# Moving the loads of the weights' chunks from SyncE's DMA queue to GpSimd's

## The chip, the cores and the metric

The kernel runs on one core of one Trainium2 chip. Its time is the device time of one execution in microseconds (us); the median of several executions counts. TensorE (PE) multiplies matrices, VectorE (DVE) and ScalarE (ACT) work on elements, GpSimd (POOL) does some element work too, and SyncE (SP) does nothing but issue DMAs. Each engine takes its instructions strictly in the order in which the program put them: an instruction that waits holds up all that stand behind it on that engine.

## What is computed

Four batches of eight attention heads (576 positions, 64 wide) with a rotation of queries and keys by position (rope), and on the attention's output, as 2304 tokens of 512, a gated layer of 1536 hidden columns:

```python
q_rot, k_rot = (rotate(q), rotate(k))
scores = scale * np.matmul(q_rot, k_rot.transpose(0, 1, 3, 2))
attn = softmax(scores); out = np.matmul(attn, v)
x = out, heads side by side: (2304, 512)
gate = 1.0 / (1.0 + np.exp(-(x @ w_gate)))
return (gate * (x @ w_val) @ w_out)
```

All is float32 at the interface. The kernel splits most operands into two float16 parts (a rounded part and what is left of it) and multiplies the parts.

## The kernel before

The weights come as 64-bit words, made of float32 pairs, that must be decoded on the chip: `w_in_chunk(f)` loads chunk f of w_gate and w_val (12 chunks, 1024 KB each) into one of three staging slots inside the tile `wo16`, decodes it with two ACT passes (`signs` L286, `low_bits` L291) and three DVE passes (`bits_1` L295, `bits_2` L298, `bits_3` L302), measures it (L324) and splits it into `w16` (L275 on ACT, L281 on DVE). `w_out_decode(f)` does the same for 12 chunks of w_out (512 KB each) through two buffers `tmp`, which lie inside `xt[1]`, the second batch's buffer.

Attention runs over a batch, four pairs of heads (p = 0 to 3) and two halves of the query rows (i = 0, 1). `keys_queries(b, p)` loads a pair's keys and queries (`x`, in the tiles `stk` for the first two batches and `qk` for the others) and the same with halves exchanged (`y`, in one of two tiles `sw`), and rotates them by two multiplications and an addition (L416, L418, L420) for each of keys and queries: on DVE for batches 0 and 1, on POOL for batches 2 and 3. `softmax` takes scores from PE (L470 for the first two batches), scales and reduces them on DVE (L505), exponentiates on ACT (L510), takes reciprocals (L513, L515) and splits the result into `p16` (L275, L281). SP then transposes `p16` into `pt` by a DMA (L537), for the last 64 rows after a small copy (L534), and PE multiplies `pt` with the values into `pv` (L547). ACT and DVE take `pv` into `xt` (L275, L281), and DVE reduces `xt` to a maximum (L556). `hidden(b, f, i)` multiplies the tokens in `xt` with a chunk of `w16` (L598), `project` with w_out (L632).

All 12 chunks of w_in and the attention of batch 0 must be done before PE can run the rest without pause: with the second half of batch 0 (i = 1) the multiplications of L598 become 320 columns wide, and the first of these marks the end of the opening.

The order on every engine is written by `Plan`. Each step is a task with an engine, a cost, a rank, and the names of what it reads and writes; a task that reads or writes a name waits in the plan for the task that last wrote it. `Plan.order` runs a list schedule over these costs, always the ready task of least rank on the engine that is free first, and the instructions are then emitted in that sequence. The waits on the chip are put in separately, from the tiles that instructions touch: a name in the plan sets only the order. A DMA is a task of SP with 0.45 us (`dma`, L224) that lands after a bus time; `port` is the plan's model of what DVE and POOL may not do at once. The first three loads of w_in and the first two of w_out need nothing but free slots.

Of the kernel before, what the change touches and what calls it, by code (L numbers as in the profile page):

```python
# [13 lines left out]
I32 = mybir.dt.int32  # L14
# [20 lines left out]
class Plan:  # L35
# [27 lines left out]
    def order(self):  # L63
        N = len(self.tasks)
        succ = [[] for _ in range(N)]
        left = [len(p) for p in self.preds]
        for n, p in enumerate(self.preds):
            for m in p:
                succ[m].append(n)
        free, wait, ready, done = {}, {}, {}, [None] * N  # L70

        def offer(n):
            for e, _ in self.tasks[n][0]:
                t = 0.0
                for m in self.preds[n]:
                    e0, end, land = done[m]
                    t = max(t, end if e0 == e and not land else end + land + self.HOP)
                heapq.heappush(wait.setdefault(e, []), (t, self.tasks[n][1], n))
                ready.setdefault(e, [])
                free.setdefault(e, 0.0)  # L80

        for n in range(N):
            if not left[n]:
                offer(n)
        starts, bus, port = [], 0.0, 0.0
        while len(starts) < N:
            best = None
            for e in free:
                w, r = wait[e], ready[e]
                while w and done[w[0][2]]:  # L90
                    heapq.heappop(w)
                while r and done[r[0][1]]:
                    heapq.heappop(r)
                if r or w:
                    t = free[e] if r else max(free[e], w[0][0])
                    if best is None or t < best[0]:
                        best = (t, e)
            t, e = best
            w, r = wait[e], ready[e]
            while w and w[0][0] <= t:  # L100
                _, rank, n = heapq.heappop(w)
                if not done[n]:
                    heapq.heappush(r, (rank, n))

            held = e in ("DVE", "POOL") and port > t + 0.2
            fit = [x for x in r if not held or (e == "DVE" and not self.tasks[x[1]][4])]
            if fit:
                x = min(fit)
                r.remove(x)
                heapq.heapify(r)  # L110
            else:
                x = heapq.heappop(r)
            n = x[1]
            where, rank, fn, land, locks = self.tasks[n]
            cost = dict(where)[e]
            if e == "POOL" or (e == "DVE" and locks):
                t = max(t, port)
                port = t + cost
            if land:

                bus = max(bus, t + cost) + land[0]
                done[n] = (e, t + cost, bus + land[1] - t - cost)
            else:
                done[n] = (e, t + cost, 0.0)
            free[e] = t + cost
            starts.append((t, n, e))
            for m in succ[n]:
                left[m] -= 1
                if not left[m]:
                    offer(m)  # L130
        self.done = done
        return sorted(starts)
# [24 lines left out]
def rope_attention_then_sigmoid_glu(ctx: ExitStack, tc: tile.TileContext, qk, v, w_in, w_out, tables, out):  # L157
    nc = tc.nc
    V, A, G, T, Y = nc.vector, nc.scalar, nc.gpsimd, nc.tensor, nc.sync
# [29 lines left out]
    tmp = [xt[1].rearrange("p c a n -> p (c a n)").bitcast(I32)[:, 1152 * n:1152 * n + 1152] for n in range(2)]  # L189
# [18 lines left out]
    P = Plan()  # L208
# [15 lines left out]
    def dma(rank, reads, writes, kb, fn, also=()):  # L224
        P.add((("SP", 0.45),), rank, reads, writes, lambda _: fn(), land=(kb / 280, 1.6), also=also)

    def transpose(rank, reads, writes, us, fn):
        P.add((("SP", 1.3),), rank, reads, writes, lambda _: fn(), land=(us, 1.2))

# [77 lines left out]
    def w_in_chunk(f, rank):  # L307
        slot = ring("stage", 3)
        tok = [("wo", 4 * slot + n) for n in range(4)]
        t = stage[slot]  # L310
        hi, lo = t[:, :, 1], t[:, :, 0]
        dst = w16[:, f].rearrange("p g a c n -> p g a (c n)")
        sg = w16[:, f, 1].rearrange("p a c n -> p (a c n)").bitcast(I8)[:, 1024:2048]
        W = ("w", f)
        dma(rank - 0.15, [], tok, 1024, lambda: Y.dma_start(out=t.rearrange("p n w -> p (n w)"), in_=w_in[f].bitcast(I32)))
        op("ACT", c_act(1024), rank, tok, [W], lambda E: signs(sg, hi))
        op("ACT", c_act(1024), rank, [], tok, lambda E: low_bits(lo))
        op2(0.7, rank, [W], tok, lambda E: bits_1(hi, hi))
        op2(c_dve(1024, two=True), rank, [], tok, lambda E: bits_2(hi, lo))
        op2(c_dve(1024, two=True), rank, [W], tok, lambda E: bits_3(hi, sg))  # L320
        r = hi.bitcast(F32).rearrange("p (g n) -> p g n", g=2)
        M = ("wm", f)
        for g in range(2):
            op("ACT", c_act(512) + 0.2, rank, tok, [M, W], lambda E, g=g: A.activation(  # L324
                dst[:, g, 0], r[:, g], AF.Abs, accum_out=w_m[:, f, g:g + 1]))
        place = m_place()
        top = allsum(rank, w_m[:, f], 2, place, [M])
        pow2(rank, top, w_s[:, f], w_i[:, f], 14, [place[1]], [("ws", f)])
        for g in range(2):
            op("ACT", c_act(512), rank, tok + [("ws", f)], [W], lambda E, g=g: scaled(  # L330
                A, dst[:, g, 0], r[:, g], w_s[:, f, g:g + 1]))
        for g in range(2):
            op2(c_dve(512, two=True), rank, tok + [("ws", f)], [W], lambda E, g=g: rest(
                dst[:, g, 1], r[:, g], w_s[:, f, g:g + 1], dst[:, g, 0]))
# [6 lines left out]
    def w_out_decode(f, rank):  # L341
        o, tok = wo_slot(f)
        n = f % 2
        X = ("tmp", n)
        XT = [("xt", 1, p, i) for p in (0, 1) for i in range(2)] if n == 0 else [("xt", 1, p, i) for p in (2, 3) for i in range(2)]
        words = tmp[n][:, 0:1024].rearrange("p (n w) -> p n w", w=2)
        hi, lo, sg = words[:, :, 1], words[:, :, 0], tmp[n][:, 1024:1152].bitcast(I8)
        dma(rank - 0.05, [], [X] + XT, 512, lambda: Y.dma_start(out=tmp[n][:, 0:1024], in_=w_out[f].bitcast(I32)))
        op("ACT", c_act(512), rank, [], [X], lambda E: signs(sg, hi))
        op("ACT", c_act(512), rank, [], [X], lambda E: low_bits(lo))  # L350
        op2(0.4, rank, [X], [tok], lambda E: bits_1(o, hi))
# [47 lines left out]
    def keys_queries(b, p, rank):  # L399

        z = ring("sw", 2)
        Z = [("sw", z, m) for m in range(2)]
        if b < NW:
            x, X = qk0[p], [("stk", n) for n in range(8 * p, 8 * p + 8)]
            X = [X[0:4], X[4:8]]
# [3 lines left out]
        y = sw[z]  # L409
        early = -8.5 if b == p == 0 else rank - 0.1  # L410
        dma(early, [], X[0] + X[1], 576, lambda: Y.dma_start(out=x, in_=qk[b, p, 0]))
        dma(early, [], Z, 576, lambda: Y.dma_start(out=y, in_=qk[b, p, 1]))
        gate = ["tab"] + ([("ws", 8 + p)] if b == 1 else [])
        places = [("POOL", c_pool(S, two=True))] if b > 1 else [("DVE", c_dve(S, two=True))]
        for m in range(2):
# [349 lines left out]
```

## Time and profile before

| | |
|---|---|
| median of 3 runs | 740.73 us (736.84 to 741.0) |
| the profiled execution | 738.06 us, of it 736.2 us span from the first to the last instruction |
| PE busy | 632.9 us (86%) |
| DVE busy | 525.1 us (71%) |
| ACT busy | 461.7 us (63%) |
| POOL busy | 74.9 us (10%) |
| DMA | one hardware queue (SP's): 99.77 MB |

The shares are means over two very different stretches: the opening up to about 207.8 us, and all that comes after. Busy times by stretch and the waits by engine are therefore read apart. A wait is shown as the idle time of an engine before an instruction with what ended it.

### The profile page before, as it was taken

The page shows a single profiled execution, that of the slowest core. Times are in us where ns is not written, and L with a number is a line of the kernel's source. Part 1 is how long each engine was busy: PE and PEld are TensorE (multiplying, and loading weights), DVE is VectorE, ACT ScalarE, POOL GpSimd, SP SyncE. Part 2 cuts the span into 40 slices and gives each one's busy share as a digit, 9 for nine tenths or more (in the row PEclk, how much of TensorE's full clock was granted, in tenths as well). Part 3 has the DMA queues.
Part 4 walks back from the last instruction along what each step waited for, and adds up shares of the span by engine and source line. Part 5 has one row for each costly group of instructions (what it writes and reads, how often), then busy time and mean ns, then how long its engine had stood idle before and what let it go on. Part 6 is the DMA issues. An engine that isn't in the chain of part 4 may idle for free.

```text
span 736.2 us, 12433 instructions
## 1 busy us (share of the span) xinstructions
PE 632.9 (86%) x4642; PEld 414.9 (56%) x4642; DVE 525.1 (71%) x1194; ACT 461.7 (63%) x940; POOL 74.9 (10%) x54
## 2 busy tenths in 40 slices
PE   2366885773199999999999899999999999999997
PEld 1134563451066644677556665587567756866753
DVE  6998899989978963787589987669968655321310
ACT  3767899876557983776666877667567655322320
POOL 0400000000033000014313022130500000000000
PEclk9999797896589999999999999999999999999999
DMA  9965744747924283387775596755774516000001
GB/s 365 316 153 133 233 154 151 195 120 203 246 83 129 52 189 93 94 187 163 160 186 134 108 202 179 165 125 119 178 152 100 131 37 151 1 1 29 1 7 37
DMA packets 187484, 100.55 MB, mean 137 GB/s; under 512 B 171040, under 2 KB 176288, under 8 KB 185376
## 3 DMA queue, kind: packets, MB, share of 16 engines
q1 hardware_dynamic: 187424, 99.77, 53.4%
q8 instruction: 36, 0.59, 0.3%
q14 instruction: 24, 0.20, 0.1%
HBM read 43.12 MB, written 4.72 MB: 65 GB/s over the span
## 4 chain that ended last, share of the span: by engine, by line
PE 69%; DVE 21%; DMA 5%; issue 3%; ACT 2%; SPq 0%; DVEq 0%; ACTq 0%
PE m L598 31%; PE m L632 19%; PE pv L547 8%; PE s L470 5%; PE s L482 4%; DVE p L281 4%; DMA pt<-p 4%; DVE p L505 3%; DVE wo L298 2%; DVE wo L302 2%; DVE w L281 1%; DVE stk L420 1%; DVE gt L281 1%; DVE sw L418 1%; DMA sw<-in_qk_dram 1%
## 5 line engine op out<-in xcount | busy, mean ns | idle before, releaser
L598 PE MATMUL m<-xt,w 128*128 128x320 f16 (+1 forms) x2304 | 302.2, 290 | 7.7 <-DVE th L608 3.5
L598 PEld LDWEIGHTS <-w 128*128 128x128 f16 x2304 | 224.6, 99 | 78.3 <-issue 14.6
L632 PE MATMUL m<-wo,gt 128*128 128x512 f16 x648 | 145.5, 379 | 1.6 <-DVE th L608 1.6
L510 ACT ACTIVATE p<-p,st 128x576 f32<-128x576 f32 x144 | 110.5, 768 | 55.5 <-DVE p L505 47.9
L281 DVE SCALAR_TENSOR_TENSOR p<-p,st,p 128x576 f16<-128x576 f32 x144 | 120.8, 868 | 21.0 <-ACT p L275 20.3
L470 PE MATMUL s<-stk 64*128 64x288 f32 (+1 forms) x320 | 70.8, 514 | 51.6 <-DVE p L505 37.2
L275 ACT ACTIVATE p<-p,st 128x576 f16<-128x576 f32 x144 | 104.4, 765 | 15.6 <-DMA pt<-p 6.4
L632 PEld LDWEIGHTS <-gt 128*128 128x128 f16 x648 | 62.4, 98 | 75.0 <-issue 5.8
L547 PE MATMUL pv<-pt,v 128*64 128x256 f16 (+3 forms) x960 | 77.2, 311 | 21.4 <-DMA pt<-p 21.4
L608 DVE SCALAR_TENSOR_TENSOR th<-th,m 128x256 f32<-128x256 f32 (+1 forms) x96 | 42.9, 450 | 68.0 <-PE m L598 65.3
L275 ACT ACTIVATE gt<-th,c_s 128x256 f16<-128x256 f32 (+1 forms) x96 | 50.3, 529 | 52.6 <-DVE th L608 51.9
L547 PEld LDWEIGHTS <-v 128*64 128x64 f16 (+1 forms) x960 | 54.6, 118 | 44.1 <-issue 30.0
L470 PEld LDWEIGHTS s<-stk 64*128 64x128 f32 (+1 forms) x320 | 35.6, 211 | 76.3 <-DVE p L505 46.8
L604 ACT ACTIVATE th<-m,gsc 128x256 f32<-128x256 f32 (+1 forms) x96 | 47.5, 494 | 41.1 <-PE m L598 40.9
L281 DVE SCALAR_TENSOR_TENSOR gt<-th,c_s,gt 128x256 f16<-128x256 f32 (+1 forms) x96 | 51.6, 542 | 18.5 <-ACT gt L275 18.3
L505 DVE TENSOR_SCALAR_CACHE_REDUCE p<-s 128x576 f32<-128x576 f32 x72 | 53.4, 750 | 15.1 <-PE s L470 14.6
L505 DVE TENSOR_SCALAR_CACHE_REDUCE p<-s,q_e 128x576 f32<-128x576 f32 x72 | 57.0, 811 | 9.8 <-PE s L482 9.3
L418 POOL TENSOR_TENSOR sw<-sw,tab 128x576 f32<-128x576 f32 x16 | 24.1, 1504 | 253.4 <-DMA sw<-in_qk_dram 222.9
L482 PE MATMUL s<-stk 128*128 128x288 f16 (+1 forms) x320 | 44.4, 287 | 3.1 <-DVE p L505 3.0
L416 POOL TENSOR_TENSOR qk<-qk,tab 128x576 f32<-128x576 f32 x16 | 25.3, 1607 | 201.7 <-DMA qk<-in_qk_dram 179.1
L482 PEld LDWEIGHTS <-stk 128*128 128x128 f16 (+1 forms) x320 | 27.5, 100 | 16.7 <-issue 8.2
L275 ACT ACTIVATE o<-m,o_s 128x512 f32<-128x512 f32 x16 | 10.9, 684 | 37.2 <-PE m L632 37.0
(94 smaller groups left out, 506.9 us busy)
## 6 DMA issues: line engine op xcount, KB each, us to landing
wo<-in_w_dram SPq DMA_DIRECT2D x12, 1024.0 KB, 5.6
sw<-in_qk_dram SPq DMA_DIRECT2D x16, 576.0 KB, 5.0
xt<-in_wo_dram SPq DMA_DIRECT2D x12, 512.0 KB, 4.7
stk<-in_qk_dram SPq DMA_DIRECT2D x8, 576.0 KB, 4.6
xt<-in_v_dram SPq DMA_DIRECT2D x4, 1152.0 KB, 7.1
qk<-in_qk_dram SPq DMA_DIRECT2D x8, 576.0 KB, 5.8
out_dram<-o SPq DMA_DIRECT2D x16, 256.0 KB, 2.0
stk<-sw SPq DMA_DIRECT2D x16, 216.0 KB, 3.5
```

Source lines behind the costliest of these rows:

```text
L275: A.activation(o, src, AF.Copy, scale=scale)
L281: V.scalar_tensor_tensor(out=o, in0=src, scalar=scale, in1=hi, op0=ALU.mult, op1=ALU.subtract)
L418: either(places, rank, gate, [Z[m]], lambda E, m=m: E.tensor_tensor(out=y[:, m], in0=y[:, m], in1=tab[:, 1], op=ALU.mult))
L470: T.matmul(s_ps[to[e]][hs if width == 64 else slice(0, 128), c, 0:288], lhsT=qT[hs, rows:rows + width], rhs=kT[hs, c * 288:c * 288 + 288], ...
L482: T.matmul(o[:, c, 0:288], lhsT=q[:, rows:rows + width], rhs=kk[:, c * 288:c * 288 + 288], start=(m == 0), stop=(m == 1))
L505: lambda E, h=h, c=c: V.tensor_scalar(out=p32[prs[c]].rearrange("p (c n) -> p c n", c=2), in0=s_ps[h][:, :, 0:288], scalar1=down, scalar2= ...
L510: lambda E, c=c: A.activation(p32[prs[c]], p32[prs[c]], AF.Exp, bias=st[:, k, 0, c:c + 1], scale=-1.0, accum_out=st[:, k, 1, c:c + 1]))
L547: T.matmul(v_ps[64 * e:64 * e + 64, 0:n], lhsT=v16[hs, p, a, g, :], rhs=pt[z][hs, c * 9 + g, 0:n], start=(first and m == 0), stop=(last an ...
L598: T.matmul(m_ps[m][:, 0:n], lhsT=w16[:, f, g, a, cc, :], rhs=x[:, cc, c, c0:c0 + n], start=(k == 0), stop=(k == 11))
L604: op("ACT", c_act(n), rank - 0.05, [("m", m), ("gsc", b, f)], [("th", r)], lambda E, m=m: A.activation(t, m_ps[m][:, 0:n], AF.Tanh, scale= ...
L608: op("DVE", c_dve(n, psum=True), rank - 0.05, [("m", m)], [("th", r)], lambda E, m=m: V.scalar_tensor_tensor(out=t, in0=t, scalar=1.0, in1 ...
L632: T.matmul(m_ps[m], lhsT=gt[:, f, a, c0:c0 + 128], rhs=wo16[:, f, c, :], start=(f == 0 and k == 0), stop=(f == NF - 1 and k == 2))
```

## The change

The 12 loads of w_in and the 12 of w_out leave SP's queue; GpSimd issues them. A new helper `load` gives them to POOL in the plan at a cost of 1.0 us, and the rule of `port` leaves them out. In addition the first three loads of w_in read a new name `("raw", 0)`, which the loads of batch 0's `sw` now write. The name is one for all four pairs of a batch, so that each of these loads in the plan also follows the landing of the one before.

```diff
-            if e == "POOL" or (e == "DVE" and locks):
+            if (e == "POOL" and not land) or (e == "DVE" and locks):
...
+    def load(rank, reads, writes, kb, fn):
+        P.add((("POOL", 1.0),), rank, reads, writes, lambda _: fn(), land=(kb / 280, 1.6))
...
-        dma(rank - 0.15, [], tok, 1024, lambda: Y.dma_start(out=t.rearrange("p n w -> p (n w)"), in_=w_in[f].bitcast(I32)))
+        load(rank - 0.15, [("raw", 0)] if f < 3 else [], tok, 1024, lambda: G.dma_start(out=t.rearrange("p n w -> p (n w)"), in_=w_in[f].bitcast(I32)))
...
-        dma(rank - 0.05, [], [X] + XT, 512, lambda: Y.dma_start(out=tmp[n][:, 0:1024], in_=w_out[f].bitcast(I32)))
+        load(rank - 0.05, [], [X] + XT, 512, lambda: G.dma_start(out=tmp[n][:, 0:1024], in_=w_out[f].bitcast(I32)))
...
-        dma(early, [], Z, 576, lambda: Y.dma_start(out=y, in_=qk[b, p, 1]))
+        dma(early, [], Z + [("raw", b)], 576, lambda: Y.dma_start(out=y, in_=qk[b, p, 1]))
```

The lines of the changed kernel are numbered 4 higher from L224 on. Three places show what it does to the order.

POOL at its start. In the kernel before, POOL went from its two memsets straight to the first rotations of batch 2 (`qk_74`, `qk_75`) and then to the rest of that rotation. In the changed kernel (`xt_65` is `xt[1]`, `wo_62` is `wo16`):

```order
L655 MEMSET zero 128x1
L656 MEMSET ones 128x128
L352 DMA xt_65<-in_wo_dram 128x1024 x2
L420 ISA
L420 TENSOR_TENSOR qk_74<-qk_74,tab 128x576 x2
L420 TENSOR_TENSOR qk_75<-qk_75,tab 128x576 x2
L319 DMA wo_62<-in_w_dram 128x2048 x12
L352 DMA xt_65<-in_wo_dram 128x1024 x10
L422 TENSOR_TENSOR sw_76<-sw_76,tab 128x576
```

Two loads of w_out are now the first DMAs of POOL, all 12 of w_in stand behind four multiplications that need batch 2's `qk`, and the other ten of w_out follow in one row.

DVE at its start. `stk` holds the rotated pairs, `sw_76` and `sw_77` are the two `sw`, `s_112` and `s_113` the scores in PSUM. Before:

```order
L420 TENSOR_TENSOR stk<-stk,sw_76 128x576
L416 TENSOR_TENSOR stk<-stk,tab 128x576 x2
L418 TENSOR_TENSOR sw_77<-sw_77,tab 128x576
L420 TENSOR_TENSOR stk<-stk,sw_77 128x576
L418 TENSOR_TENSOR sw_77<-sw_77,tab 128x576
L420 TENSOR_TENSOR stk<-stk,sw_77 128x576
L505 TENSOR_SCALAR p_78,st<-s_112 128x576
L505 TENSOR_SCALAR p_79,st<-s_113 128x576
L416 TENSOR_TENSOR stk<-stk,tab 128x576 x2
L505 TENSOR_SCALAR p_80,st<-s_112 128x576
```

and now:

```order
L424 TENSOR_TENSOR stk<-stk,sw_76 128x576
L420 TENSOR_TENSOR stk<-stk,tab 128x576 x2
L509 TENSOR_SCALAR p_78,st<-s_112 128x576
L509 TENSOR_SCALAR p_79,st<-s_113 128x576
L517 TENSOR_SCALAR st<-st 128x2
L519 RECIPROCAL st<-st 128x2
L509 TENSOR_SCALAR p_80,st<-s_112 128x576
L420 TENSOR_TENSOR stk<-stk,tab 128x576 x3
```

The four steps with pair 1's `sw_77` no longer stand between pair 0's rotation and its softmax, since the load of `sw_77` now comes later on SP; the small steps on `st`, which need both exponentials, follow the two reductions at once.

SP in the opening. Before, the queue after its first transposes reads:

```order
L537 DMA_TRANSPOSE pt_72<-p_81 128x18x128
L315 DMA wo_62<-in_w_dram 128x2048
L537 DMA_TRANSPOSE pt_72<-p_82 128x18x128
L537 DMA_TRANSPOSE pt_71<-p_81 128x18x128
L537 DMA_TRANSPOSE pt_71<-p_82 128x18x128
L315 DMA wo_62<-in_w_dram 128x2048
```

and now:

```order
L541 DMA_TRANSPOSE pt_72<-p_81 128x18x128
L541 DMA_TRANSPOSE pt_72<-p_82 128x18x128
L541 DMA_TRANSPOSE pt_71<-p_81 128x18x128
L541 DMA_TRANSPOSE pt_71<-p_82 128x18x128
L415 DMA stk<-in_qk_dram 128x1152
```

The transposes have no load of a weight between them any more. Up to the eighth and last `xt<-pv` of batch 0 on DVE (the step that ends the opening), the changed order puts one decode of a w_out chunk (L295, L298 and L302 in the 512-wide form: 11 of each for 10) and one L418 (15 for 14) more ahead of that step than before; all other counts up to there are equal, and PE's matrix multiplications up to its first 320-wide L598 are the same in kind and number.

## Rows read from the trace of the kernel before

**Rows 1.** Windows: stretch, its length, each engine's busy us (instructions), PEclk, DMA, GB/s
```profile
6.20:40.00 33.80, 13.64 (x38) 7.17 (x38) 31.32 (x54) 20.38 (x38) 7.47 (x4) 1.00 0.94 339
40.00:207.80 167.80, 104.99 (x700) 69.68 (x700) 152.79 (x323) 129.40 (x266) 0.00 (x0) 0.81 0.65 180
207.80:736.20 528.40, 514.30 (x3908) 338.02 (x3906) 341.01 (x818) 310.46 (x636) 66.94 (x44) 1.00 0.48 109
```
**Rows 2.** Waits of DVE, 0 to 207.8: total us, times, longest
```profile
DVE stk L416 <- DMA stk<-in_qk_dram: 6.2, 1, 6.2
DVE xt L281 <- ACT xt L275: 5.8, 5, 2.4
```
**Rows 3.** SP's first DMA issues in the timeline (start us, us)
```profile
0.74 0.40 SPq L655 DMA_DIRECT2D tab<-in_const_dram  x1
1.20 0.41 SPq L411 DMA_DIRECT2D stk<-in_qk_dram  x1
...
6.14 3.55 SPq L315 DMA_DIRECT2D wo<-in_w_dram  x3
...
10.75 3.06 SPq L348 DMA_DIRECT2D xt<-in_wo_dram  x2
```
**Rows 4.** Windows again, 6.2 to 26 us: the last number is GB/s
```profile
6.20:26.00 19.80, 7.64 (x22) 4.07 (x22) 18.32 (x36) 10.14 (x21) 0.00 (x0) 1.00 1.02 421
```
**Rows 5.** Timeline around the first softmax (start us, us; idle before in brackets)
```profile
10.85 1.42 DVE L416 TENSOR_TENSOR stk<-stk,tab 128x576 f32<-128x576 f32 x2
...
10.98 2.29 PE L470 MATMUL s<-stk 64*128 64x288 f32 x8 [10.98 <-DVE stk L420]
...
15.78 0.75 DVE L505 TENSOR_SCALAR_CACHE_REDUCE p<-s 128x576 f32<-128x576 f32 x1
...
17.42 0.76 ACT L510 ACTIVATE p<-p,st 128x576 f32<-128x576 f32 x1
```
**Rows 6.** DVE's groups by form, 0 to 207.8: count, busy us, mean ns, idle before
```profile
L281 DVE SCALAR_TENSOR_TENSOR p<-p,st,p 128x576 f16<-128x576 f32 x36 | 29.3, 844 | 0.2 <-ACT p L275 0.2
...
L418 DVE TENSOR_TENSOR sw<-sw,tab 128x576 f32<-128x576 f32 x14 | 10.5, 751 | 0.3 <-DMA sw<-in_qk_dram 0.3
...
L298 DVE SCALAR_TENSOR_TENSOR wo<-wo,xt 128x512 int32<-128x512 int32 x10 | 6.9, 692 | 0.9 <-ACT xt L291 0.4
L302 DVE SCALAR_TENSOR_TENSOR wo<-wo,xt 128x512 f32<-128x512 f32 x10 | 6.9, 687 | 0.2
...
L295 DVE TENSOR_SCALAR wo<-xt 128x512 int32<-128x512 int32 x10 | 4.2, 418 | 0.0
```
**Rows 7.** Timeline, 50 to 66 us: a load, the transposes behind it, PE and DVE
```profile
52.30 0.43 SPq L315 DMA_DIRECT2D wo<-in_w_dram  x1
...
61.59 3.55 PE L547 MATMUL pv<-pt,v 128*64 128x256 f16 x30 [3.26 <-DMA pt<-p]
...
65.59 0.42 DVE L281 SCALAR_TENSOR_TENSOR xt<-pv,xt 128x256 f16<-128x256 f32 x1 [2.36 <-ACT xt L275]
```
**Rows 8.** Timeline at the end of the opening: SP, then PE
```profile
193.04 0.53 SPq L348 DMA_DIRECT2D xt<-in_wo_dram  x1
...
193.68 0.62 SPq L534 DMA_DIRECT2D p<-p  x1
...
207.85 1.80 PE L598 MATMUL m<-xt,w 128*128 128x320 f16 x12
```
**Rows 9.** POOL and DVE side by side in the timeline
```profile
27.97 7.47 POOL L416 TENSOR_TENSOR qk<-qk,tab 128x576 f32<-128x576 f32 x4 [27.00 <-DMA qk<-in_qk_dram]
...
29.52 2.30 DVE L298 SCALAR_TENSOR_TENSOR wo<-wo 128x1024 int32<-128x1024 int32 x1
...
34.09 2.69 DVE L281 SCALAR_TENSOR_TENSOR p<-p,st,p 128x576 f16<-128x576 f32 x2
```
**Rows 10.** Line L298 alone: ns min/median/max, first and last start
```profile
L298 DVE SCALAR_TENSOR_TENSOR wo<-wo x12: 1210/1226/2302, 29.5 to 145.1; 128x1024 int32<-128x1024 int32 x12
```
**Rows 11.** The loads of w_in: DMA issue to landing, us
```profile
DMA to landing us min/median/max: 4.8/5.6/14.6
```

## The prediction, made before the changed kernel ran

> **What bounds the kernel now.** I read the busy times by stretch first, since the loads that move are all issued before PE's first 320-wide product at 207.85 [rows 8]. Behind it PE is busy for 514.30 of 528.40 us [rows 1]: that part is PE at its limit, it has none of the moved loads in it, and the order shows the same products ahead of this point in both kernels. So I take its 528.40 us as unchanged, and the question is when the opening ends. There PE is busy for only 104.99 of 167.80 us, while DVE is busy for 152.79 of them, and for 31.32 of the 33.80 before [rows 1]. The opening is DVE's. Second I read DVE's waits: until 207.8 it waits for a DMA directly only at the very start, 6.2 us for the first keys, queries and table, and the next largest wait is 5.8 us in five pieces for ACT's part of `xt`, which stands behind the transposed probabilities [rows 2]. No wait of DVE there is for a weight's load: the loads were not late for it. What SP's queue cost is therefore at most what its transposes come late by, and most of that is hidden already, as DVE is busy with other work.
>
> **The change, term by term.** All against the profiled execution's own 738.06 us (736.2 of span and 1.86 around it); it lies 2.7 us under the median of the runs shown and inside their scatter.
>
> *The head.* Before, the two early loads of w_out were issued at 10.75, behind everything that batch 0 needs [rows 3]. Now POOL issues them as its first DMAs, next to SP's table at 0.74 and first `stk` at 1.20 [rows 3], though ACT is the only one to use them early and nothing on DVE needs them for tens of us. They are 2 x 0.524 = 1.05 MB; at the 421 GB/s that the DMA engines moved from 6.2 to 26 us [rows 4] that is 2.5 us. If both queues are served side by side, all of it stands ahead of the `stk` for which DVE starts: 2.5 us. If service follows the order of issue, only the first load does: 1.25 us. If POOL needs longer to issue than these first landings take, nothing: 0. No row shows a DMA of POOL. I take 1.9, the middle of the two cases in which it issues promptly, and keep 0 to 2.5. The Trainium skill, "DMA: Bandwidth & Descriptors", section on queues, rings and completion order, says that each DMA engine takes turns between the queue rows that have work, packet by packet; by that rule the term would be the upper 2.5 and the sum 0.6 higher. No run here shows it yet.
>
> *The first softmax.* Pair 1's `sw` is loaded later, so four DVE steps (4 x 0.75 us, L418 and L420) go from between pair 0's rotation and its softmax. They were a cover. In the times of the rows [rows 5]: the multiplication of pair 1 that still precedes it ends at 10.85 + 1.42 = 12.27, the scores at 10.98 + 2.29 = 13.27, so DVE waits 1.0. Behind the second reduction (end 15.78 + 0.75 = 16.53) now come L513 and L515, which need the second exponential; that ended at 17.42 + 0.76 = 18.18, 1.65 later. Before, a rotation step filled this. Sum 2.7 us of new idle time. The load of pair 3's `sw` now also runs close to its use; I set that against the 2.5 us that DVE idled from 6.2 to 40 (33.80 - 31.32, [rows 1]), of which some belongs to places that are gone, and price neither. Range 1 to 5.
>
> *The order.* Ahead of the step that ends the opening DVE now has one 512-wide decode more, 0.418 + 0.692 + 0.687, and one L418 of 0.751 [rows 6]: 2.55 us. That work is not new, but where it stood before, PE was the bound and it cost nothing.
>
> *SP's free queue.* This is the gain. The load issued at 52.30 stood ahead of transposes for which PE then waited 3.26 us and DVE, at 65.59, 2.36 us [rows 7]. At 193.04 a load of w_out stood ahead of the small copy that could be issued only at 193.68, and PE started the 320-wide products late [rows 8]. The five waits of DVE of this kind make 5.8 us [rows 2]: no more can come back by this way. The loads still share the DMA engines with the transposes, so not all does. I take 4.0; range 2 to 5.8.
>
> *POOL beside DVE.* The four multiplications on `qk` stretched DVE: from 27.97 on, a decode step took 2.30 us where 1.21 is its least, its twin the same, and two splits 2.69 where 2 x 0.844 is their mean [rows 9, 10, 6], 3.2 us in all. They now come earlier, as `qk` no longer queues behind five weight loads, and meet rotations and splits instead. Same POOL time, same kind of partner: 0, range -2 to +1. Issuing 24 DMAs on POOL itself costs POOL nothing that anyone waits for, since from 35.4 to 207.8 it had no work [rows 1, 9]. The wait behind which w_in now stands is POOL's own order: no load starts before `qk` has landed and four multiplications of 1.87 us are done. Counted as in the order term (steps by their mean durations), DVE first touches a chunk some 34 us of its own work into the order, against 21 before, so it should be there.
>
> Sum: 738.06 + 1.9 + 2.7 + 2.55 - 4.0 = 741.2; I say **741 us**, 0.4% over the profiled execution, level with the median.
>
> **The rivals.**
>
> *POOL's issuing takes DVE's time (slower).* Rows 9 show that a POOL instruction working beside DVE's two-input steps costs DVE: 3.2 us for four instructions, 0.8 each. If writing a DMA's descriptors blocks DVE likewise, 22 loads in the opening cost up to 22 x 0.8 = 17.6 us: 759. At half, 750. It decides (over 1%) from 0.3 us per load on. For it: DVE is busy 91% of the opening, so hardly an issue goes by it in silence. Against: issuing moves few bytes through SBUF, multiplying 128x576 floats three streams of them.
>
> *SP's freedom is worth more (faster).* From 40 to 207.8 DVE idles 167.80 - 152.79 = 15.0 us. If most of this is a tail of late transposes (PE behind them, ACT behind PE), 12 may come back, and the head may cost nothing: 738.06 + 2.7 + 2.55 - 12 = 731. For it: the waits of L281 stand in a chain with PE's 3.26 and DVE's 2.36. Against: only 5.8 of the 15.0 name that chain.
>
> *The loads come late (a new wait).* A load took 4.8 to 14.6 us to land [rows 11]. If POOL issues and lands each slower by a few us, ACT stands before `signs`, and behind it on ACT the exponentials; DVE then waits for both. With 3 us at two or three of the loads, 741 + 7 = 748. For it: the ten late loads of w_out stand in one row with two buffers. Against: POOL has nothing else to do and issues as soon as a buffer is free, where SP had a queue. The Trainium skill, "SBUF — State Buffer", section on who interferes with whom, states that while DVE runs certain modes GpSimd cannot write a DMA's descriptors, so that the DMA seems blocked by DVE. By that rule each load would wait out DVE's current step, and this rival is how it would show. No run here has a POOL DMA to agree or differ.
>
> *The gate does nothing.* The reading of `("raw", 0)` only moves the first three loads in the plan; on the chip no wait follows from it. They come behind `qk` either way. This changes no number of mine, and is in the forecast.
>
> **How the numbers follow.** Forecast with its terms at their ends: low 738 + 0 + 1 + 2.5 - 2 - 5.8 = 734, high 738 + 2.5 + 5 + 2.55 + 1 - 2 = 747: chance 0.60. POOL blocks DVE: 0.15, 748 to 759. Faster: 0.18, 727 to 733. Late loads: 0.07, about 748, on either side of the bound. About 1% (7.4 us) is what a measurement of this kernel tells from no change. Faster by over 1%: 0.18. Slower by over 1%: 0.15, and 0.08 from the late loads and the upper end of the forecast: 0.23. Within: 0.59. For 8 in 10 I cut the outer halves of both rivals: 731 to 752.
>
> **What the changed profile would show.** Head: DVE's first step at about 8.1 instead of 6.2 (right), at 6.2 (term is nil). First softmax: idle times of about 1.0 before the first L505 (now L509) and 1.7 before L513 (now L517). Order and SP: the first 320-wide L598 (now L602) near 211, DVE's waits for `xt` together under 2 us, transposes issued within a microsecond of the splits they need. From there to the end 528 us again; if that part differs by more than 3 us, my cut at 207.8 is wrong. POOL as a blocker: DVE's two-input steps with several over their least duration, at the times of POOL's issues. Late loads: waits of ACT for `in_w` or `in_wo` ahead of the exponentials, or of DVE for them. The forecast is wrong if the opening ends before 202 or after 218.

## The result

| | before | after |
|---|---|---|
| median | 738.77 us (736.84 to 741.79, 11 runs) | 744.26 us (743.02 to 750.0, 11 runs) |
| profiled execution, its span | 738.06, 736.2 us | 745.5, 743.7 us |

The changed kernel takes 1.0079 times as long, 95% interval 1.0054 to 1.0103: slower by 0.8%, inside the 1% that the prediction counted as no change, 3.3 us above its 741. The number held, by luck: its composition, as the experiments show, did not.

The three windows of the kernel after, cut as [rows 1] (the first 320-wide product now starts at 217.60):

```profile
6.20:40.00 33.80, 8.68 (x28) 4.75 (x28) 25.87 (x42) 14.01 (x28) 8.60 (x7) 1.00 0.85 316
40.00:217.60 177.60, 109.90 (x709) 72.56 (x709) 161.50 (x337) 137.92 (x280) 12.03 (x21) 0.76 0.65 175
217.60:743.70 526.10, 513.35 (x3908) 336.98 (x3906) 340.59 (x816) 308.95 (x630) 65.88 (x43) 1.00 0.48 109
```

The opening is 9.75 us longer, the rest 2.3 us shorter: together the 7.5 us between the spans. (In the new order ten of these first products stand ahead of the last `xt`. Cut at DVE's last step on `xt`, at 207.26 and 219.36, the opening is 12.1 us longer and the rest 4.6 us shorter.) Of the 9.75, DVE is busy for 3.3 (161.50 and 25.87 and none before 6.2 make 187.4, against 184.1) and idle for 6.5. Its waits up to 217.6, beside [rows 2]:

```profile
DVE sw L422 <- DMA sw<-in_qk_dram: 6.9, 2, 4.3
DVE stk L420 <- DMA stk<-in_qk_dram: 6.2, 1, 6.2
DVE st L517 <- ACT p L514: 2.8, 3, 1.0
DVE p L509 <- PE s L474: 2.7, 5, 1.0
DVE xt L285 <- ACT xt L279: 2.1, 2, 1.4
DVE w_i L243 <- PE m L268: 1.9, 3, 1.3
DVE w L285 <- ACT w L279: 1.4, 1, 1.4
DVE th L612 <- PE m L602: 1.0, 3, 0.4
```

Before, the same waits were 0.3 for `sw`, 6.2 for `stk`, 0.4 for `st`, 1.7 for `p`, 5.8 for `xt`, 0.7 for `w_i`, none for `w` and 3.3 for `th`. So `sw` is +6.6, `st` +2.4, `p` +1.0, `w_i` +1.2, `w` +1.4, `xt` -3.7, `th` -2.3: 6.6 in all, the idle time that was gained. The largest entry, two waits for a load of `sw`, stands in the timeline of DVE like this (start, us, and the idle time before in brackets):

```profile
6.19 1.43 DVE L420 TENSOR_TENSOR stk<-stk,tab 128x576 f32<-128x576 f32 x2 [6.19 <-DMA stk<-in_qk_dram]
10.21 0.76 DVE L422 TENSOR_TENSOR sw<-sw,tab 128x576 f32<-128x576 f32 x1 [2.59 <-DMA sw<-in_qk_dram]
...
15.60 0.76 DVE L509 TENSOR_SCALAR_CACHE_REDUCE p<-s 128x576 f32<-128x576 f32 x1 [1.04 <-PE s L474]
...
18.06 0.17 DVE L517 TENSOR_SCALAR st<-st 128x2 f32<-128x2 f32 x1 [1.01 <-ACT p L514]
...
42.46 0.76 DVE L422 TENSOR_TENSOR sw<-sw,tab 128x576 f32<-128x576 f32 x1 [4.30 <-DMA sw<-in_qk_dram]
```

The step at 10.21 is the head, where the kernel before started it at 7.91. The one at 42.46 is pair 3's `sw`. The DMA issues show why it is late, POOL's and then SP's:

```profile
26.21 1.64 POOL L319 DMA_DIRECT2D wo<-in_w_dram  x3
```
```profile
29.84 7.56 SPq L541 DMA_TRANSPOSE pt<-p  x1
37.51 0.98 SPq L416 DMA_DIRECT2D sw<-in_qk_dram  x2
```

POOL issues three loads of w_in (3.1 MB) from 26.21 on; behind them one transpose keeps SP for 7.56 us, and only then can SP issue pair 3's load of 576 KB, for which DVE has been standing since 38.2. The trace's page lists POOL's loads as a queue of another kind than SP's `hardware_dynamic`:

```profile
q0 software_dynamic: 3456, 18.88, 7.7%
```

That is packets, MB, and the share of the DMA engines' time.

### The profile page after: what moved, and what is told of

The parts are those of the page before. It is cut to its first block, busy times and chain, and to the rows that moved or that the text cites. A ratio compares the mean times of both kernels' runs of the same rounds, so it can differ in the third digit from the quotient of the medians.

```text
span 743.7 us, 12442 instructions
## 1 busy us (share of the span) xinstructions
PE 631.9 (85%) x4642; PEld 414.3 (56%) x4642; DVE 528.0 (71%) x1194; ACT 462.4 (62%) x940; POOL 88.2 (12%) x78
## 3 DMA queue, kind: packets, MB, share of 16 engines
HBM read 43.12 MB, written 4.72 MB: 64 GB/s over the span
## 4 chain that ended last, share of the span: by engine, by line
PE 69%; DVE 14%; DMA 4%; issue 3%; ACT 3%; DVEq 0%; ACTq 0%
PE m L602 34%; PE m L636 17%; PE pv L551 7%; PE s L474 4%; PE s L486 4%; DMA pt<-p 4%; DVE p L285 3%; DVE p L509 2%; DVE wo L302 2%; DVE wo L306 1%; DVE wo L299 1%; ACT p L279 1%; DVE sw L422 1%; DVE stk L420 1%; DVE stk L424 1%
## 5 line engine op out<-in xcount | busy, mean ns | idle before, releaser
L285 DVE SCALAR_TENSOR_TENSOR p<-p,st,p 128x576 f16<-128x576 f32 x144 | 119.1, 856 | 23.2 <-ACT p L279 22.6
L608 ACT ACTIVATE th<-m,gsc 128x256 f32<-128x256 f32 (+1 forms) x96 | 47.4, 495 | 38.2 <-PE m L602 37.8
L285 DVE SCALAR_TENSOR_TENSOR gt<-th,c_s,gt 128x256 f16<-128x256 f32 (+1 forms) x96 | 54.7, 575 | 17.9 <-ACT gt L279 17.5
```

The costliest lines, as they stand in the source:

```text
L285: V.scalar_tensor_tensor(out=o, in0=src, scalar=scale, in1=hi, op0=ALU.mult, op1=ALU.subtract)
L608: op("ACT", c_act(n), rank - 0.05, [("m", m), ("gsc", b, f)], [("th", r)], lambda E, m=m: A.activation(t, m_ps[m][:, 0:n], AF.Tanh, scale= ...
```

## Experiments

The planner answers any edit with another order on all engines, so an edit alone mixes two causes. Six kernels therefore keep an order, row for row on DVE, ACT, PE and SP, and change only who issues a load or when; the rest change the plan. No kernel leaves out any of the computation. Ratios are to the kernel before as timed on the same chip in that set of runs (its medians were 738.77 to 739.65 us), so they are not quotients of the column of medians; "eighth xt" is the start of DVE's eighth step `xt<-pv`, the last one that the 320-wide products wait for, and "behind it" is the span from there to the end, both of the profiled execution.

| kernel | median us | ratio (95%) | eighth xt | behind it |
|---|---|---|---|---|
| before | 738.77 | 1 | 207.26 | 528.9 |
| after | 744.26 | 1.0079 (1.0054 to 1.0103) | 219.36 | 524.3 |
| after's order, SP issues | 738.06 | 0.9990 (0.9964 to 1.0015) | 212.68 | 525.6 |
| after's order, w_in truly gated | 741.97 | 1.0012 (0.9982 to 1.0042) | 211.25 | 523.0 |
| the same, w_out gated too | 740.23 | 1.0020 (0.9994 to 1.0045) | 214.40 | 524.1 |
| before's order, POOL issues | 748.67 | 1.0109 (1.0063 to 1.0155) | 216.76 | 529.1 |
| names per pair | 746.83 | 1.0117 (1.0079 to 1.0155) | 218.62 | 522.9 |
| names per pair, w_out behind them | 731.75 | 0.9899 (0.9863 to 0.9935) | 202.82 | 526.6 |
| its order, w_out first | 736.58 | 0.9964 (0.9931 to 0.9996) | 212.43 | 525.4 |
| its order, SP issues | 731.88 | 0.9893 (0.9857 to 0.9929) | 205.76 | 525.8 |
| its plan, one cost nudged | 733.26 | 0.9945 (0.9916 to 0.9974) | 209.84 | 526.0 |
| no name at all | 755.23 | 1.0216 (1.0179 to 1.0254) | 227.21 | 526.9 |
| before, loads planned behind all sw | 735.85 | 0.9967 (0.9942 to 0.9992) | 206.74 | 526.8 |
| before, one cost nudged | 737.93 | 0.9987 (0.9960 to 1.0013) | 211.62 | 526.2 |

TensorE's granted clock, as a mean over an execution and a share of the higher of its two levels (2.4 GHz), goes from 0.934 to 0.958 in executions of the kernel before, so it could stand behind any of these differences. It does not make the two main ones. The changed kernel ran at 0.934 to 0.945 and the same order on SP at 0.938 to 0.946, and PE's busy time ahead of the first 320-wide product is 118.6 us in both kernels' profiles (13.64 + 104.99 and 8.68 + 109.90). The kernel of 731.75 us ran at 0.950 to 0.955, and executions of the kernel before at 0.946 or more have medians of 738.2 to 739.4. Differences of a few us are not safe from it: with w_in truly gated, four executions at 0.946 or more have a median of 738.1 us, seven below 742.7.

Theory A, held first, was that the loss comes of the order: the shared name chains the loads of `sw`. Theory B was that GpSimd's queue costs.

**Order alone.** The plan of the change, with the loads issued by SP:

```diff
-        load(..., lambda: G.dma_start(out=t..., in_=w_in[f]...))
+        load(..., lambda: Y.dma_start(out=t..., in_=w_in[f]...))
```
(and the same for w_out)

> The changed kernel's plan with its order of instructions on every engine, but SyncE issues the loads again. Theory A: the order costs as before the change of queue, SyncE's transposes also stand behind loads again (3.7 us of DVE's waits for xt come back): the opening ends at 217 to 224, time 744 to 750. Theory B (GpSimd's queue is what costs): 737 to 740, with the opening ending at 207 to 211.

B's time came, 738.06, level with before; but the opening, up to 213.74, is longer than B's and shorter than A's. The windows say how both can be:

```profile
0.00:213.70 213.70, 123.27 (x736) 79.84 (x736) 189.21 (x383) 154.62 (x312) 10.63 (x12) 0.78 0.68 203
213.70:738.30 524.60, 513.09 (x3908) 337.35 (x3906) 339.46 (x813) 308.06 (x629) 63.33 (x43) 1.00 0.49 109
```

The eighth `xt` is 5.4 us later than before, and what comes behind is shorter: PE's idle time there falls from 14.1 us (528.40 - 514.30, [rows 1]) to 11.5 (524.60 - 513.09). That work taken into the opening is work that PE does not wait for later would fit this, but no wait was followed that far. What the table shows is that the stretch behind goes with the order: 528.9 and 529.1 us in the order of before on either queue, 523.0 to 525.6 in the four kernels with after's order. This kernel is also not free of the head: SP now issues the two early loads of w_out at 1.20 and 3.00, and DVE's first step on `sw` starts at 9.16 instead of 7.91. And DVE's waits in this kernel hold the next surprise:

```profile
DVE xt L285 <- ACT xt L279: 1.4, 4, 0.6
```

Most of the 5.8 us of [rows 2] is gone with SP issuing every load. It is the order that removes it, not the free queue.

**Queue alone.** The kernel before in its own order, POOL issuing; one copied column of pair 1's `sw` ahead of the first load keeps POOL from starting too early.

```diff
+        if f == 0:
+            G.tensor_copy(out=late, in_=sw[1][:, 0, 0:1])
-        Y.dma_start(out=t..., in_=w_in[f]...)
+        G.dma_start(out=t..., in_=w_in[f]...)
```

> The kernel before with its order on DVE, ACT, PE and SyncE kept, but GpSimd issues all loads of weights; ahead of the first it copies one column of pair 1's sw, so that none starts before that has landed (at about 8 to 10 us, where SyncE issued the first at 6.1). This is the change of queue alone. If SyncE's freedom gives the 4 us of the prediction: DVE's waits for xt fall from 5.8 to about 2 us, the opening ends at 203 to 206, time 733 to 737. If it gives nothing, since the waits for xt belong to the order: they stay at 4 to 6 us, opening 207 to 209, time 738 to 741. If GpSimd's queue costs as such: opening 211 or later, time 742 to 746.

It is 1.1% slower, and the waits for `xt` rise:

```profile
DVE xt L282 <- ACT xt L276: 8.6, 6, 2.6
```

The two kernels keep within 1 us of each other up to the third `xt` (77.71 and 78.57); the largest single step, from 1.8 us at the fourth to 5.7 at the fifth, comes at 144. SP's timeline before, around that place, and its landing of the copy `p<-p` (issues, KB, median us):

```profile
128.75 0.73 SPq L534 DMA_DIRECT2D p<-p  x1
129.59 0.53 SPq L315 DMA_DIRECT2D wo<-in_w_dram  x1
131.58 1.59 SPq L537 DMA_TRANSPOSE pt<-p  x1
```
```profile
p<-p SPq DMA_DIRECT2D x1, 144.0 KB, 2.8
```

and the same with POOL issuing, the timeline of SP, of POOL, of PE and of DVE, then the landing:

```profile
131.07 0.73 SPq L540 DMA_DIRECT2D p<-p  x1
138.27 1.29 SPq L543 DMA_TRANSPOSE pt<-p  x1
```
```profile
131.19 0.53 POOL L311 DMA_DIRECT2D wo<-in_w_dram  x1 [8.52 <-DVE w_i L242]
```
```profile
141.91 1.81 PE L553 MATMUL pv<-pt,v 128*64 128x320 f16 x12 [4.72 <-DMA pt<-p]
```
```profile
144.28 0.16 DVE L240 TENSOR_SCALAR w_i<-m 128x2 f32<-128x2 f32 x1 [3.50 <-PE m L265]
```
```profile
p<-p SPq DMA_DIRECT2D x1, 144.0 KB, 7.2
```

On one queue the 1 MB load stood behind the copy of 144 KB. On two it starts 0.1 us after it and shares the DMA engines with it; the copy lands after 7.2 us instead of 2.8, the transpose that reads it starts 6.7 us later on the clock (2.3 of them were lost before the copy was issued), PE waits 4.72 us where it waited 1.50, and DVE 3.5, where it did not wait, for a sum that stands behind that product. The Trainium skill, "DMA: Bandwidth & Descriptors", section on queues, rings and completion order, has each DMA engine take turns between queue rows, a packet at a time; the 2.8 and 7.2 us agree with that. This place makes 3.9 of the 9.5 us by which the eighth `xt` is late; the smaller steps were not followed.

So a third theory, Q: **the queue of SP kept large loads from overtaking or accompanying small transfers for which DVE waits; POOL's queue does not, and that is all it costs.**

**A gate that waits.** After's order; POOL copies a column of pair 3's `sw` ahead of the first load of w_in.

```diff
+        if f == 0:
+            G.tensor_copy(out=late, in_=sw[1][:, 0, 0:1])
         G.dma_start(out=t..., in_=w_in[f]...)
```

> The changed kernel, its order on every engine kept, with one GpSimd instruction more: ahead of the first load of w_in GpSimd copies one column of the sw tile that pair 3 is loaded into, so that the three loads of w_in truly wait for that landing. Theory Q (the loss against the same order with SyncE issuing, 744.3 against 738.1, is that GpSimd issues three loads of 1.05 MB ahead of a small load that DVE waits for): DVE's wait for pair 3's sw falls from 4.3 us to under 1, the opening ends at 212 to 215 instead of 217.6, time 738 to 741. Rival H (the loss is at the head, or is a price of GpSimd's queue as such): 743 to 746, the opening still ends at 216 to 218.

POOL's timeline, SP's, and DVE's wait for `sw` up to 209.4:

```profile
35.92 0.22 POOL L314 COPY late<-sw 128x1 f32<-128x1 f32 x1 [9.96 <-DMA sw<-in_qk_dram]
36.39 1.64 POOL L315 DMA_DIRECT2D wo<-in_w_dram  x3 [0.24 <-issue]
```
```profile
28.51 2.03 SPq L547 DMA_TRANSPOSE pt<-p  x1
```
```profile
DVE sw L428 <- DMA sw<-in_qk_dram: 1.6, 1, 1.6
```

Loads ten us later, and the kernel is faster: the first transpose keeps SP for 2.03 us instead of 7.56, the wait of 4.3 is gone, the ratio falls from 1.0079 to 1.0012. (The next transpose now takes 8.16 us, at 41.98, but none of batch 0's keys and queries stands behind it.) The median, 742, is above the 738 to 741 expected (the profiled execution is one of its two shortest, so its 211.25 flatters it), but the interval covers 1. That the ratio after the gate cannot be told from that of SP issuing (0.9990) leaves little for any other price of the queue in this order. The times of one order on both queues say the same. The first step `xt<-pv` on DVE in the changed kernel, with SP issuing, and with the gate:

```profile
62.65 0.42 DVE L285 SCALAR_TENSOR_TENSOR xt<-pv,xt 128x256 f16<-128x256 f32 x1
```
```profile
57.01 0.42 DVE L285 SCALAR_TENSOR_TENSOR xt<-pv,xt 128x256 f16<-128x256 f32 x1
```
```profile
56.94 0.42 DVE L286 SCALAR_TENSOR_TENSOR xt<-pv,xt 128x256 f16<-128x256 f32 x1
```

The changed kernel is 5.6 us late here and stays 4.6 to 6.7 late up to the eighth `xt`: nearly all that the queue costs is lost by here. With SP issuing, the first step on `sw` and the first on pair 3's stand so:

```profile
9.16 0.76 DVE L422 TENSOR_TENSOR sw<-sw,tab 128x576 f32<-128x576 f32 x1
...
36.82 0.75 DVE L422 TENSOR_TENSOR sw<-sw,tab 128x576 f32<-128x576 f32 x1
```

In the changed kernel they start at 10.21 and 42.46: of the 5.6 us, 4.3 are the wait for pair 3's `sw`, and 1.05 the head. The gated kernel has the changed kernel's first loads and yet starts that step at 9.12, so the part at the head is within what two executions differ by. Open is whether a second queue of SP's kind would cost the same: no run put the loads on one.

**Both gates.** The same, and POOL's first loads of w_out wait for the table:

```diff
+        if f == 0:
+            G.tensor_copy(out=late, in_=tab[:, 0, 0:1])
         G.dma_start(out=tmp[n][:, 0:1024], in_=w_out[f]...)
```

> The changed kernel, its order kept on DVE, ACT, PE and SyncE, with two gates on GpSimd: one column of the table is copied ahead of the first load of w_out (so that it starts at about 5 us instead of 1.3), one column of pair 3's sw ahead of the first of w_in. Theory Q (nothing but loads that start ahead of, or beside, small transfers for which DVE waits makes GpSimd's queue cost): the head's wait for sw falls from 1.6 to under 0.7 us, the opening is at least 1 us shorter than with the one gate, time 736 to 740, level with the same order on SyncE (738.1). Rival (GpSimd's queue costs some us as such, by the later loads): 741 to 744, as with the one gate (742.0).

The time is that of one gate, 740.23, and the opening is not shorter: a miss. The wait for `sw` at the head falls to 0.7 as expected, but ACT now waits for w_out ahead of the exponentials, and DVE for ACT (DVE's waits, 0 to 60 us):

```profile
DVE st L528 <- ACT p L525: 6.0, 3, 4.2
```

That is the rival "the loads come late", made real: 3.2 us more there ate the 0.9 at the head.

**Names per pair.** The load of each `sw` writes a name of its own, the first three of w_in read all four; in the second kernel the first two loads of w_out read them as well.

```diff
-        dma(early, [], Z + [("raw", b)], 576, ...)
+        dma(early, [], Z + [("raw", b, p)], 576, ...)
-        load(rank - 0.05, [], [X] + XT, 512, ...)
+        load(rank - 0.05, [("raw", 0, p) for p in range(NP)] if f < 2 else [], [X] + XT, 512, ...)
```

> The changed kernel with one edit: each pair's load of sw writes a name of its own, and the first three loads of w_in read all four names. The three sw loads behind the first are no longer chained by the shared name, so they are planned early as before the change, and pair 1's rotation stands between pair 0's scores and its softmax again; GpSimd still issues all loads of weights, two of w_out at the very start. Theory A (the loss is in the first 60 us and comes of the order that the shared name forces: pair 3's sw late behind a transpose and the three w loads, and the softmax without its cover): the 4.3 us before pair 3's sw and the 2.4 us at the first softmax go, the head's 2.3 us stay; the opening (up to PE's first 320-wide product) ends at 209 to 212 instead of 217.6, time 736 to 739. Theory B (the loss is the price of GpSimd's queue itself: slower landing, GpSimd beside DVE): the opening still ends at 215 to 218, time 743 to 746.

> The same as the kernel with a name for each pair's sw, and also the first two loads of w_out read the four names, so that GpSimd issues nothing before its multiplications on qk. Theory A: the head's 2.3 us (DVE's first step on sw at 10.2 instead of 7.9) come back too; the opening ends at 207 to 210, time 734 to 737, 1.5 to 2.5 us under the kernel with the names alone. Theory B: the head is not what costs, time 742 to 746. If the first ACT work on w_out becomes late by this, ACT waits for xt before the exponentials and the time is no better than that of the kernel with the names alone.

A misses by 8 us on the first and is beaten on the second, where B misses by 10. Taking the chain away does not repair the loss; 15 us lie between two kernels whose edits differ by what two loads read, and whose orders differ all over. The next run keeps the second's order and issues these two loads first again, beside POOL's memsets:

```diff
+        for n in range(2):
+            G.dma_start(out=tmp[n][:, 0:1024], in_=w_out[n]...)
```

> The kernel with the names for each pair and the gated loads of w_out (731.75 us), its order kept on DVE, PE, ACT and SyncE, but the first two loads of w_out are GpSimd's first DMAs again, as in the changed kernel. It prices the head alone. If the head costs what the first landings show (DVE's step on sw at 9.2 to 10.2 instead of 7.9): 1.3 to 2.3 us more, opening at 205 to 206, time 733 to 734.5. If the 15 us between this kernel and the one with the names alone (746.8) are the head's: 740 to 747. If they are the planner's, which put nearly every engine in another order for that edit, the first case holds.

736.58: 4.8 us, neither 2 nor 15. The step on `sw` is late by 1.33 at the start, DVE still by 1.0 to 1.9 at the sixth and seventh `xt`; then a transpose takes longer than in the faster kernel. SP's timeline of the faster kernel, SP's of this one, and this one's DVE:

```profile
183.83 5.04 SPq L541 DMA_TRANSPOSE pt<-p  x1
```
```profile
185.70 8.37 SPq L541 DMA_TRANSPOSE pt<-p  x1
```
```profile
192.21 0.82 DVE L285 SCALAR_TENSOR_TENSOR p<-p,st,p 128x576 f16<-128x576 f32 x1 [3.78 <-ACT p L279]
203.03 0.43 DVE L299 TENSOR_SCALAR wo<-xt 128x512 int32<-128x512 int32 x1 [2.00 <-DMA xt<-in_wo_dram]
```

A microsecond at the head has become 9.6 at the end of this execution's opening (which is slower than its median); that the one led to the other is argued, not shown. Against the kernel with the names alone this one differs in nothing but the order: 746.83 - 736.58, 10 us, are the planner's, and what in the order costs them was not followed.

The faster kernel's order with SP issuing (`Y.dma_start` for `G.dma_start` in both loads):

> The kernel with the names for each pair and the gated loads of w_out (731.75 us), its order kept on every engine, with SyncE issuing the loads at their places in that order. If order alone makes it fast: 730 to 733. If GpSimd's queue is what makes it fast, as the transposes no longer stand behind loads: 734 to 740, DVE's waits for xt above 4.6 us. If GpSimd's queue costs (as it does in the changed kernel's order, 6.2 us): 725 to 729.

731.88 against 731.75: in this order the queue costs nothing that can be told. POOL's loads of w_in start behind its multiplications at 24.38, when all four `sw` had been issued or stood ahead of the transposes.

**No name at all**, so that three loads of w_in and two of w_out are POOL's first work:

```diff
-        load(rank - 0.15, [("raw", 0)] if f < 3 else [], tok, 1024, ...)
+        load(rank - 0.15, [], tok, 1024, ...)
```

> The changed kernel without the name through which the first three loads of w_in stand behind the landing of sw. GpSimd then issues three loads of w_in (3 x 1.05 MB) and two of w_out (2 x 0.52 MB) as its first work, 4.2 MB beside the table, stk and sw. If transfers of the two queues share the DMA engines evenly until GpSimd's are done: sw and stk of the first pairs land up to 4.2 MB / 421 GB/s = 10 us late, DVE's first steps start at 12 to 18, opening ends at 214 to 220, time 742 to 748. If GpSimd's queue is slow to start (about 0.5 us for each issue was seen later on) and SyncE's loads go first: DVE's second step near 10 as in the changed kernel, the order of before without the late sw of pair 3, opening ends at 207 to 211, time 735 to 739.

The slowest, by 2.2%: DVE's step on `sw` starts at 11.65, less than the worst bound, but the opening lasts to 226. Its order is another one again, so the split between head and order stays open.

**Is the faster kernel an accident of its order?** Three runs: a planner's cost of 0.46 us for 0.45 in the kernel before, the same in the faster kernel, and the kernel before with the five loads reading the four names on SP.

```diff
-        P.add((("SP", 0.45),), rank, reads, writes, ...)
+        P.add((("SP", 0.46),), rank, reads, writes, ...)
```
```diff
-        dma(rank - 0.15, [], tok, 1024, ...)
+        dma(rank - 0.15, [("raw", 0, p) for p in range(NP)] if f < 3 else [], tok, 1024, ...)
```

> The kernel before with one cost of the planner nudged: a DMA's issue on SyncE is put at 0.46 us instead of 0.45. Nothing of substance changes, but the planner's ties fall otherwise and the order moves on all engines (833 rows of difference on DVE). It measures how far a mere other order moves the time. If orders of this planner are all alike: 737 to 741. If the order alone is worth several us, as the kernels with names for each pair suggest (746.8 and 731.9 by orders that differ): anything from 730 to 750, the opening ending 5 us or more away from 207.8.

> The kernel with names for each pair and gated loads of w_out (731.75 us, loads by GpSimd), with the same nudge of the planner as above, 0.46 us for 0.45. If its speed is due to the gates: 729 to 735. If it was the luck of one order: 736 to 746.

> The kernel before, all loads on SyncE, where the first three loads of w_in and the first two of w_out read the names of the four sw loads, so that the planner puts them behind the keys and queries of batch 0; no load goes to GpSimd in the plan or on the chip. If it is the place of these loads in the plan that makes the kernel with gated loads fast (731.75 on GpSimd, 731.88 on SyncE): 729 to 734, the opening ending at 202 to 206. If that speed was the luck of one order: 736 to 745.

The nudge moves the kernel before by nothing that can be told (0.9987) and the faster one from 0.9899 to 0.9945; the gates on SP give 0.9967, a median of 735.85 that falls between its two cases. The three orders in which the early loads stand behind the keys and queries are 0.3, 0.6 and 1.0% faster than before. The kernel with names per pair and w_out behind them, 731.75 us, beats both kernels, by 1.0 and 1.8% (0.9899 / 1.0079 = 0.982); by the nudged kernel's ratio about half of its lead over before hangs on one order.

## Why the prediction was right, and where not

The total was right, the terms were not. It had order at +5.25 (softmax 2.7, order 2.55) and queue at -2.1 (head 1.9, SP -4.0). Timed apart, the order comes to nothing (738.06 - 738.77 = -0.7, inside its interval) and the queue to +6.2 (744.26 - 738.06). The two errors cancel but for 3 us; that the total was right is luck. So it is that the opening kept its bound: the first 320-wide product starts at 217.60, under the 218 named, but the last `xt` only at 219.36.

*The head, +1.9.* DVE's first step is at 6.19, not at 8.1: `stk` was not delayed, it landed after 4.9 us in both kernels. `sw` landed after 8.5 us instead of 6.2, and the step on it was late by 2.3. The size is that of the upper bound, the place one load further on; why `stk`, issued 0.1 us ahead of POOL's first load, was spared, no run shows.

*The first softmax, +2.7.* Nearly right: 1.04 and 1.01 make 2.05 (a third wait there, 0.32, is not new: it was 0.36).

*The order, +2.55.* With the softmax 5.25 was forecast for the opening and 5.4 measured with SP issuing, but the two agree by luck: the 5.4 hold a head of 1.25 and 4.4 us less of waits for `xt`. Wrong as a cost: the step that failed is "where it stood before, PE was the bound and it cost nothing". With it the cut at 207.85 failed, by which the rest was to be 528.40 in both; it is 526.10, and 524.60 with the order alone. The prediction allowed it 3 us: from the first 320-wide product the difference is 2.3, from the last `xt` 4.6.

*SP's free queue, -4.0.* The size came (`xt` waits 5.8 to 2.1), the cause was another. The order alone removes them; the queue alone raises them to 8.6. [Rows 7] showed a load ahead of transposes, and I read the wait behind it as the load's; with SP's queue freed of it, in the same order, that wait is still 2.4 us:

```profile
66.34 0.42 DVE L282 SCALAR_TENSOR_TENSOR xt<-pv,xt 128x256 f16<-128x256 f32 x1 [2.36 <-ACT xt L276]
```

POOL then issues the same load at 53.56, so this clears the queue and not the load.

*POOL beside DVE, 0.* Four of DVE's rotations beside the multiplications took 7.46 us where 4 x 0.75 are due: 4.5 lost, against 3.2 in [rows 9]. +1.3, just past the range's end.

```profile
19.43 5.58 DVE L420 TENSOR_TENSOR stk<-stk,tab 128x576 f32<-128x576 f32 x3
25.00 1.88 DVE L420 TENSOR_TENSOR stk<-stk,tab 128x576 f32<-128x576 f32 x1
```

*Not priced: pair 3's `sw`, +4.3.* The prediction named it as running "close to its use" and set it against idle time elsewhere. It also had the loads behind POOL's multiplications as safe, asking only whether they come late. That they come at 26.21, in front of a transpose and a small load, was asked nowhere, and none of the rivals holds it.

*The rivals.* POOL's issuing does not take DVE's time: the decode step of [rows 10] now never exceeds 1.228 us (least 1.219), 24 issues notwithstanding. "The gate does nothing" is right, and was worth more than a remark: a gate that waits gives back 0.7%. Late loads are not what costs at the first softmax: ACT waits for w_out until 9.46, 7.23 us, but its first exponential at 16.40 then stands 3.08 us for DVE. By the Trainium skill's "SBUF — State Buffer", who interferes with whom, DVE can hold up POOL's DMAs, but not with every step, as the prediction had it: the section counts copies, casts and scalar steps in a two-port mode, and reports that `tensor_tensor` did not stall one. POOL's 12 issues of w_in took 0.527 to 0.597 us each and the loads landed after 6.3 us in the median, 5.6 before [rows 11], with DVE busy for 86% of the opening (187.4 of 217.6). No wait of that kind shows here, but only 3 of the 24 issues, at 88.58, 103.50 and 212.42, stood beside a wide scalar step (L299), so the rule was hardly tried.

## What to carry to other kernels

A single in-order queue is also a priority list: before moving bulk loads off it, list the small transfers that stood ahead of them and make the bulk wait for these on the chip, since a name in a planner only orders the program. Time the order and the mechanism apart, by freezing one, whenever a planner answers an edit with a new order. A wait that stands behind a load in a queue is not yet the queue's: here it stayed when the load left the queue, and went with another order.

## What the runs showed of the hardware

A transpose's issue keeps SP for 1.28 us at the least and 1.98 in the median of the changed kernel's 80, and for 7.56 or 8.37 with loads of POOL's queue in flight, so that everything behind it in SP's queue is late too. A second queue is not needed for that: the first two transposes of the kernel before, which has SP's alone, took 7.02 and 2.07 us of this row of its timeline (3.9 us lie between them),

```profile
25.91 12.97 SPq L537 DMA_TRANSPOSE pt<-p  x2
```

the first while the DMA engines moved 410 GB/s (24 to 30 us), and with after's order on SP the one at 42.05 took 8.07. POOL issues a DMA of 512 KB or 1 MB in about 0.53 us (0.527 to 0.717) with DVE busy beside it. A copy of 144 KB took 7.2 us to land instead of 2.8 when a 1 MB load was issued 0.1 us after it on another queue; that load took 6.9 instead of 5.7.
